# Sliding-window attention into a GELU layer: batch 0 loaded and worked on pair by pair, first weights in three column pieces

## The chip, the cores and the metric

The kernel runs on one core of a Trainium2 chip. Time is device time in microseconds (us) of that core. Three runs of the kernel before gave 296.78, 296.99 and 299.27 us, median 296.99. A separate execution was recorded with the profiler: it took 296.65 us, of which the recorded span of instructions is 294.6 us.

## The reference

The input is q, k and v of eight batches, eight heads, 576 positions and 64 values a head, and two weight matrices, w_in (512 x 2048) and w_out (2048 x 512), all in float32.

```python
scores = scale * np.matmul(q, k.transpose(0, 1, 3, 2))
mask = np.abs(pos[:, None] - pos[None, :]) <= 32
attn = softmax(where(mask, scores, -1e9))
attn_out = np.matmul(attn, v)                       # 8, 8, 576, 64
x = attn_out.transpose(0, 2, 1, 3).reshape(4608, 512)
out = gelu_tanh(x @ w_in) @ w_out                   # 4608, 512
```

## The kernel before, in words

**Tiles and stages.** The 4608 rows of x are worked on in nine tiles of 512 rows (`t`), and the attention of a later batch is woven between the products of an earlier tile. The products run in fp16. For tile `t`, the first product x @ w_in gives 16 blocks of 128 columns of the hidden layer (`fc`), each a sum of four matmuls of 512 columns, one for each quarter `dc` of d_model; a GELU on ScalarE follows. A quarter `dc` of x is what the pair of heads `dc` gives, so the matmuls with `dc` 0 can begin when pair 0 of the attention is done. The second product takes the hidden layer to the output.

**The start.** Nothing can be woven into the attention of batch 0, so it and the first product of tile 0 make a start of their own (lines 796 to 920). Each pair of heads passes these steps, which the code calls by name:

- `cast_early`: q and k of the pair become fp16 (VectorE for q, GpSimd for k).
- `turn` and `trans_out`: eight transposes on TensorE into PSUM banks x0 and x1, and two copies out of them (QT and KT).
- `score`: the scores of the pair, with a bias matmul that brings the mask, and one `Exp` of 128 x 1024 on ScalarE (line 481).
- `sum_up` and `invert`: the sums of the rows by a matmul with ones (line 495), then `Ln` and `Exp` on ScalarE (lines 530, 531), which give 1/sum.
- `values`: v of the pair becomes fp16 (GpSimd) and is copied once more, shifted by 64 rows (`pair_v` on VectorE, lines 225, 226).
- `times` and `spread`: the products with v (line 505), and the product with 1/sum, which writes the pair's quarter of x (line 540).

The order before is: all of q and k are loaded, then v pair by pair, then w_in; scores and sums of all four pairs go first, then `finish` (`times` and `spread`) pair by pair as v lands. `spin` issues matmuls on zeros whose result nobody reads.

**Weights of the first product.** w_in is loaded in fp32 in eight DMAs of 128 x 1024 (two column halves `x`, four quarters `dc`, line 246), becomes fp16 in casts of 512 columns (line 250) on GpSimd and ScalarE or VectorE, and is used as a view `w_cols` in which a block `fc` takes every fourth column of a group of 512. w_out's rows are loaded to match, four consecutive rows to a partition. `block_in(ns, *dcs)` issues the matmuls (line 577) of blocks `ns` for quarters `dcs`; after the last quarter come the GELUs. Before, blocks 0 to 5 are run quarter by quarter as w_in's first half arrives, then 6 and 7, then 8 to 13, then 14 and 15.

**What sets the order.** The order is written out by hand: every engine takes its instructions in the order of the program, and SP's queue, which issues nearly all loads, takes the DMAs in that order too. After line 920 a table of slots (`PLAN_0`) weaves the attention of batch 1 into the second product of tile 0 (line 723). The stage buffers (five, 8 KB a partition) are passed from v of batch 0 and the w_in pieces on to the pieces of w_out and v of batch 1, so a load of these waits for the last cast out of the buffer.

Of the kernel before, what the change touches and what calls it, by code (L numbers as in the profile page):

```python
# [9 lines left out]
FP32 = mybir.dt.float32  # L10
# [68 lines left out]
def kernel(  # L79
# [152 lines left out]
            copy(V[0:64, 3 + c, :, :], V[0:64, c, :, :])  # L232

    w_in_v = moe_w_in.rearrange("(c p) f -> p c f", p=128)
    w_out_v = moe_w_out.rearrange("(i p c) f -> i p c f", p=128, c=4)
    w_cols = w_in16.rearrange("k d (i p j) -> k d i j p", i=4, j=4)

    def stage_w():
        return stage.tile([128, 4, 512], FP32, name="wst", tag="stage")

    wi = {}

    def load_w_in(x, dc):
        if dc % 2 == 0:
            wi[x, dc // 2] = stage.tile([128, 2, 1024], FP32, name="wst", tag="stage")
        nc.sync.dma_start(wi[x, dc // 2][:, dc % 2, :], w_in_v[:, dc, 1024 * x:1024 * x + 1024])

    def cast_w_in(x, dc, *copies):
        for y, copy in enumerate(copies):
            copy(w_in16[:, dc, 1024 * x + 512 * y:1024 * x + 512 * y + 512],  # L250
                 wi[x, dc // 2][:, dc % 2, 512 * y:512 * y + 512])

    def load_w_out(i, w, c0=0, c1=4):
        nc.sync.dma_start(w[:, c0:c1, :], w_out_v[i, :, c0:c1, :])
        return w

    def cast_w(w, dst, on_dve=(0, 1), cs=range(4), on_act=()):
# [5 lines left out]
    qk(0, (nc.sync, nc.scalar))  # L263
    tails_0("k")
    qk(2, (nc.scalar, nc.sync))
    qk(4)
    qk(6)
    load_table(exp_set)
    def v_of_pair(g, hs=(0, 1)):
        for h in (2 * g + x for x in hs):  # L270
            nc.sync.dma_start(raws[0][3][:, :, h, :], v[0, h, 0:512, :].rearrange("(c p) d -> p c d", p=128))

    vs(4)
    for g in range(3):
        v_of_pair(g)
    for x in range(2):
        load_w_in(0, x)
        v_of_pair(3, (x,))
    for x, dc in ((0, 2), (0, 3), (1, 0), (1, 1), (1, 2), (1, 3)):
        load_w_in(x, dc)  # L280

    idle = KTs[1][:, 0, 0:512]
    nc.vector.memset(idle, 0.0)
# [1 line left out]
    def spin(n, width=512, ps=None):  # L285
        ps = psO.tile([128, 512], FP32, name="spin", tag="O") if ps is None else ps
        for _ in range(n):
            nc.tensor.matmul(ps[:, 0:width], idle[:, 0:128], idle[:, 0:width], start=True, stop=True)
# [43 lines left out]
    def cast_early(b, pr, engs):  # L332
        for src, dst, eng in zip(raws[b][0:2], halfs[b][0:2], engs):
            if eng is not None:
                eng.tensor_copy(dst[:, pr, :, :, :].rearrange("p j h d -> p h j d"),
                                src[:, 2 * pr:2 * pr + 2, :].rearrange("p h (j d) -> p h j d", j=4))
# [26 lines left out]
    def cast_tail_0(copy, i):  # L363
        if len(halfs[0]) < 3:
            halfs[0].append(hp.tile([128, H, 64], FP16, name="t16", tag="t16"))
        copy(halfs[0][2][:, 4 * i:4 * i + 4, :], raws[0][2][:, 4 * i:4 * i + 4, :])
# [21 lines left out]
    def trans_out(b, pr, pt, ptk, copy=nc.vector.tensor_copy):  # L388
        nc.vector.tensor_copy(QTs[b][:, pr, :, 0:128], pt[:, 0:4, :])
        copy(  # L390
            KTs[b % 2][:, pr, :].rearrange("d (p j) -> d p j", j=4),
            ptk[:, 0:4, :].rearrange("d j p -> d p j"))
# [165 lines left out]
    def ffn_in(t, n, d0=0, d1=4, then=True):  # L558
        fc = column(t, n)
        if t not in gTs:  # L560
            gTs[t] = gp.tile([128, NF, 512], FP16, name="gT", tag="gT")
        if d0 == 0:
            if t == 0:
                i = n % 8
                if i in (4, 6):
                    phs["S"] = psS.tile([128, 2, 512], FP32, name="ph2", tag=f"S{i // 2 - 2}")
                phs[fc] = psO.tile([128, 512], FP32, name="ph", tag="DO"[i]) if i < 2 else \
                    bank(i - 2) if i < 4 else phs["S"][:, i % 2, :]
            else:
                i = 3 if n in (1, 2) else 0 if n == 0 else (2, 1, 0)[n % 3] if t < NT - 2 else (2, 0)[n % 2 if n > 3 else 0]  # L570
                if n == 1:
                    phs["S"] = psS.tile([128, 2, 512], FP32, name="ph3", tag="S0")
                phs[fc] = bank(i) if i < 2 else phs["S"][:, n - 1, :] if i == 3 else \
                    psO.tile([128, 512], FP32, name="ph", tag="D")
        ph = phs[fc]
        for dc in range(d0, d1):
            nc.tensor.matmul(ph, w_cols[:, dc, fc // 4, fc % 4, :],  # L577
                             xT[:, dc, t * 512 % RING:t * 512 % RING + 512],
                             start=(dc == 0), stop=(dc == 3))
        if d1 == 4 and then:  # L580
            gelu(t, n)
# [9 lines left out]
    def in_w(eng, unit, *which):  # L591

        i, j = UNITS[unit] // 2, 2 * (UNITS[unit] % 2)
        A11, A12, A21, A22 = (w_cols[:, d:d + 2, c + i, j:j + 2, :] for c in (0, 2) for d in (0, 2))
        if (unit, "s") not in mixed:
            halves = [(rawp if unit == "A" else yp).tile([128, 2, 2, 2, 128], FP16, name="wc" + unit + str(x),
                                                         tag=("qr", "kr")[x] if unit == "A" else "yo") for x in range(2)]
            mixed[unit, "s"] = [half[:, x] for half in halves for x in range(2)]
        S1, S2, S3, S4 = mixed[unit, "s"]
        mixed[unit, "w"] = dict(A11=A11, A12=A12, A22=A22, S1=S1, S2=S2, S3=S3, S4=S4)  # L600
        for x in which:
            dst, a, b, op = ((S1, A21, A22, ALU.add), (S2, S1, A11, ALU.subtract),
                             (S3, A11, A21, ALU.subtract), (S4, A12, S2, ALU.subtract))[x - 1]
            eng.tensor_tensor(dst, a, b, op=op)
# [195 lines left out]
    def turn(g):  # L800
        pts[g] = (bank16(0), bank16(1))
        trans_pair(0, g, *pts[g], now=False)

    def pieces(tag, name):
        return psO.tile([128, 512], FP32, name=name, tag=tag) if tag in "OD" else \
            psS.tile([128, 2, 512], FP32, name=name, tag=tag)[:, 0, :]

    lts, os = {}, {}

    def sums_of(g):  # L810
        d = pieces("DO"[g % 2], "ps_d")
        sum_up(0, g, d, groups[(0, g)])
        lts[g] = invert(0, g, d)


    cast_early(0, 0, split)
    turn(0)
    trans_out(0, 0, *pts[0], nc.scalar.copy)
    cast_early(0, 1, split)
    cast_tail_0(nc.vector.tensor_copy, 1)  # L820
    spin(3)
    trans_tail_0(psO.tile([128, 8, 128], FP16, name="pt", tag="D"), 1, nc.scalar.copy)
    score(0, 0, 0)
    turn(1)
    cast_early(0, 2, split)
    trans_out(0, 1, *pts[1])
    spin(1)
    sums_of(0)
    cast_early(0, 3, split)
    turn(2)  # L830
    score(0, 1, 1)
    trans_out(0, 2, *pts[2])
    cast_vt(0)
    spin(1)
    score(0, 2, 0)
    turn(3)
    trans_out(0, 3, *pts[3])
    sums_of(1)
    score(0, 3, 1)
    sums_of(2)  # L840

    def values(g, copy):
        hs = slice(2 * g, 2 * g + 2)
        copy(Vs[0][:, 0:4, hs, :], raws[0][3][:, :, hs, :])
        pair_v(0, nc.vector.tensor_copy, hs)

    def finish(g, o):
        times(0, g, o, groups.pop((0, g)))
        spread(0, g, o, lts[g])

    values(0, nc.gpsimd.tensor_copy)
    values(1, nc.gpsimd.tensor_copy)

    qk, tails, vs = load_early(1)
    qk(0)
    wo = [load_w_out(0, stage_w())]
    qk(2)

    finish(0, bank(0))
    finish(1, bank(1))  # L860
    s0 = psS.tile([128, 2, 512], FP32, name="ps_o", tag="S0")
    spin(2, 512, s0[:, 1, :])
    sums_of(3)
    spin(2, 512, s0[:, 1, :])
    values(2, nc.gpsimd.tensor_copy)
    s1 = psS.tile([128, 2, 512], FP32, name="ps_o", tag="S1")
    finish(2, s1[:, 0, :])
    six = range(6)

    def block_in(ns, *dcs):  # L870
        for dc in dcs:
# [2 lines left out]
        if 3 in dcs:  # L874
            for n in ns:
                gelu(0, n)

    cast_w_in(0, 0, nc.gpsimd.tensor_copy, nc.scalar.copy)
    values(3, nc.vector.tensor_copy)
    block_in(six, 0)  # L880
    cast_w_in(0, 1, nc.gpsimd.tensor_copy, nc.scalar.copy)
    block_in(six, 1)
    finish(3, s1[:, 1, :])
    load_table(gelu_set)
    cast_w_in(0, 2, nc.gpsimd.tensor_copy, nc.scalar.copy)
    cast_w_in(0, 3, nc.gpsimd.tensor_copy, nc.vector.tensor_copy)
    block_in(six, 2, 3)
    band_out()
    for dc in range(4):
        cast_w_in(1, dc, nc.vector.tensor_copy, nc.gpsimd.tensor_copy)  # L890
    wo.append(load_w_out(1, stage_w()))
    qk(4)
    tails_0("q")
    wo.append(load_w_out(2, stage_w(), 0, 2))
# [10 lines left out]
    cast_open(1)  # L905
    split = (nc.gpsimd, nc.vector)

    block_in((6, 7), 0, 1, 2, 3)
    block_in(range(8, 14), 0, 1, 2, 3)
    cast_early(1, 0, split)  # L910
    cast_w(wo[0], w_out16[:, 0:4, :], (0,), (0, 2, 3, 1))
    for dc in range(4):
# [197 lines left out]
```

## Time and profile before

| what | value |
|---|---|
| runs | 296.78, 296.99, 299.27 us; median 296.99 |
| profiled execution, its own time | 296.65 us |
| its span | 294.6 us |
| TensorE matmul busy in the span | 285.9 us, 97% |
| VectorE, ScalarE, GpSimd busy | 72%, 67%, 30% |
| first useful matmul of the first product | 17.37 us |
| first matmul of the second product | 32.69 us |

The page cuts the span into 40 slices of 7.4 us. TensorE has idle time in the first three slices and in the last; from 21 us on the start is one unbroken row of matmuls. The two times in the last rows are from the timeline of TensorE and are used below as marks: everything that this change touches lies ahead of the second one, but for the order of columns in the weights.

### The profile page before, as it was taken

How to read it: one execution, taken by the hardware profiler on the slowest of the kernel's cores; microseconds unless marked ns; L12 is line 12 of the kernel's file. 1: busy time of each engine (PE TensorE's matmuls, PEld its weight loads, DVE VectorE, ACT ScalarE, POOL GpSimd, SP SyncE). 2: the span in 40 equal slices, each digit the busy share in tenths (PEclk: the TensorE clock that was granted, in tenths of full speed). 3: DMA queues.
4: the chain of work that ended last, by engine and by line, in shares of the span. 5: the costliest groups of instructions: out<-in, count | busy, mean ns of one | idle time of the engine just before them, and what ended most of it. 6: DMA issues, size and time to landing. Idle time of an engine off the chain costs nothing.

```text
span 294.6 us, 7286 instructions
## 1 busy us (share of the span) xinstructions
PE 285.9 (97%) x2945; PEld 192.7 (65%) x2945; DVE 212.4 (72%) x467; ACT 196.5 (67%) x315; POOL 88.8 (30%) x143
## 2 busy tenths in 40 slices
PE   8889999999999999999999999999999999999993
PEld 3535545547765687568755885588558867887783
DVE  4755477998897667858796878686957877865762
ACT  5965877777677874787667776796669558706800
POOL 4445335004228713205250615050800050025000
PEclk9999999999999999999999999999999999999998
DMA  7999998999999998999999999899691040004013
GB/s 229 275 380 396 359 305 196 254 186 203 248 229 202 251 202 188 113 139 245 162 212 94 246 157 191 116 245 154 117 190 7 0 118 28 2 26 120 0 47 99
DMA packets 114392, 51.02 MB, mean 173 GB/s; under 512 B 98471, under 2 KB 110247, under 8 KB 114102
## 3 DMA queue, kind: packets, MB, share of 16 engines
q1 hardware_dynamic: 89460, 38.67, 62.4%
q0 software_dynamic: 23776, 10.83, 23.4%
q10 hardware_dynamic: 1122, 1.06, 1.1%
q8 instruction: 23, 0.38, 0.6%
q14 instruction: 11, 0.09, 0.1%
HBM read 36.70 MB, written 9.44 MB: 157 GB/s over the span
## 4 chain that ended last, share of the span: by engine, by line
PE 85%; DVE 5%; DMA 5%; issue 1%; SPq 1%; ACT 1%; POOL 0%; DVEq 0%
PE mm L751 32%; PE ph L577 17%; PE mm L577 16%; PE ps_s L468 4%; PE pu L629 3%; DMA kr<-in_k_dram 3%; PE mm L723 2%; DMA wst<-in_moe_w_in_dram 2%; PE py L723 2%; PE ps_d L495 2%; PE ps_o L505 2%; DVE t L684 2%; DVE s L694 1%; PE mm L629 1%; PE ps_od L495 1%; PE ps_od L505 1%
## 5 line engine op out<-in xcount | busy, mean ns | idle before, releaser
L577 PEld LDWEIGHTS <-w_in 128*128 128x128 f16 x512 | 57.4, 113 | 49.8 <-POOL w_in L250 1.5
L577 PE MATMUL ph<-xT,w_in 128*128 128x512 f16 x256 | 64.5, 379 | 0.6 <-POOL w_in L250 0.6
L577 PE MATMUL mm<-xT,w_in 128*128 128x512 f16 x256 | 64.1, 379 | 0.0
L585 ACT ACTIVATE gT<-mm 128x512 f16<-128x512 f32 x60 | 35.6, 598 | 33.3 <-PE mm L577 32.7
L713 POOL DMA_DIRECT2D out_dram<-y x55 | 32.8, 605 | 82.4 <-DVE y L780 75.3
L751 PEld LDWEIGHTS <-s 128*128 128x128 f16 x512 | 49.3, 98 | 7.1 <-DVE s L694 0.6
L751 PE MATMUL mm<-t,s 128*128 128x256 f16 x376 | 45.2, 273 | 0.2 <-DVE y L764 0.2
L694 DVE TENSOR_TENSOR s<-gT 128x512 f16<-128x512 f16 x64 | 27.5, 430 | 19.1 <-ACT gT L585 18.9
L751 PEld LDWEIGHTS <-gT 128*128 128x128 f16 x384 | 36.2, 98 | 6.4
L585 ACT ACTIVATE gT<-ph 128x512 f16<-128x512 f32 x58 | 32.4, 604 | 10.9 <-PE ph L577 10.9
L481 ACT ACTIVATE pe<-ps_s 128x960 f16<-128x960 f32 (+1 forms) x31 | 29.5, 975 | 13.2 <-PE ps_s L468 13.1
L751 PE MATMUL mm<-w_out,gT 128*128 128x256 f16 x256 | 32.6, 273 | 0.0
L104 ACT ACT_TABLE_LOAD x18 | 23.1, 1283 | 2.2 <-issue 1.9
L530 ACT ACTIVATE lt<-ps_d 128x480 f32<-128x480 f32 (+2 forms) x28 | 15.6, 556 | 10.4 <-PE ps_d L495 6.9
L531 ACT ACTIVATE lt<-lt 128x480 f32<-128x480 f32 (+3 forms) x36 | 21.1, 585 | 1.1
L490 DVE TENSOR_TENSOR pe<-pe,band 128x960 f16<-128x960 f16 x28 | 18.5, 680 | 2.0 <-ACT pe L481 1.9
L505 PEld LDWEIGHTS <-V 128*64 128x64 f16 x520 | 13.7, 111 | 5.5 <-DVE V L226 1.5
L751 PE MATMUL mm<-t,gT 128*128 128x256 f16 x128 | 16.1, 273 | 0.0
L694 DVE TENSOR_TENSOR s<-s,gT 128x512 f16<-128x512 f16 x32 | 14.0, 436 | 1.1
L216 POOL DMA_DIRECT2D V<-in_v_dram x16 | 14.3, 908 | 1.1 <-PE ps_s L468 0.4
L751 PE MATMUL mm<-w_out,s 128*128 128x256 f16 x120 | 14.6, 273 | 0.0
L540 DVE TENSOR_TENSOR xT<-ps_o,lt 128x480 f16<-128x480 f32 (+5 forms) x26 | 13.4, 535 | 1.6 <-PE ps_o L505 1.6
(149 smaller groups left out, 390.3 us busy)
## 6 DMA issues: line engine op xcount, KB each, us to landing
kr<-in_k_dram SPq DMA_DIRECT2D x31, 256.0 KB, 10.2
qr<-in_q_dram SPq DMA_DIRECT2D x6, 1024.0 KB, 5.9
wst<-in_moe_w_in_dram SPq DMA_DIRECT2D x8, 512.0 KB, 6.6
wst<-in_moe_w_out_dram SPq DMA_DIRECT2D x2, 1024.0 KB, 10.5
wst<-in_moe_w_out_dram SPq DMA_DIRECT2D x4, 512.0 KB, 7.4
qr<-in_v_dram SPq DMA_DIRECT2D x8, 256.0 KB, 6.5
V<-in_v_dram POOLq DMA_DIRECT2D x16, 128.0 KB, 8.5
qr<-in_q_dram SPq DMA_DIRECT2D x7, 256.0 KB, 7.3
```

Of the source, the lines that this page charges most:

```text
L104: nc.scalar.add_instruction(mybir.InstLoadActFuncSet(name=nc.get_next_instruction_name(), act_func_set_id=which, ins=[], outs=[]))
L216: nc.gpsimd.dma_start(V[:, c, :, :], v[b, :, 128 * c:128 * c + 128, :].rearrange("h p d -> p h d"))
L481: nc.scalar.activation(pe, ps[:, :, 0:w], AF.Exp, scale=SCALE)
L490: nc.vector.tensor_tensor(pe, pe, m.rearrange("k (o j) p -> k o j p", o=1).broadcast_to(list(pe.shape)), op=ALU.mult)
L505: nc.tensor.matmul(o[64 * h:64 * h + 64, cols].rearrange("d (j p) -> d j p", j=4)[:, :, p0 - q0:p1 - q0], Vs[b % 2][:, slot, 2 * pr + h, : ...
L530: nc.scalar.activation(lt[:, 0:n], d[:, 0:n], AF.Ln)
L531: nc.scalar.activation(lt[:, 0:n], lt[:, 0:n], AF.Exp, scale=-1.0)
L577: nc.tensor.matmul(ph, w_cols[:, dc, fc // 4, fc % 4, :], xT[:, dc, t * 512 % RING:t * 512 % RING + 512], start=(dc == 0), stop=(dc == 3))
L585: nc.scalar.activation(gTs[t][:, fc, :], phs[fc], AF.Gelu_apprx_tanh)
L694: nc.vector.tensor_tensor(dst, x, y, op=op)
L713: eng.dma_start(out_v[b, j, q0 + p:q0 + p + e, cols], yo[m:m + e, cols])
L751: nc.tensor.matmul(pys["apart"][:, 0:256] if apart else py[:, blk, :], lhsT, wino[w][:, f, :], start=(new and i % (8 if one else 16) == 0) ...
```

## The change

**Loads.** v of pair 0 (and the last 64 rows of v) is now issued ahead of q and k of pair 2, v of pair 1 ahead of q and k of pair 3. The form of the loads of v, one row to a partition, stands in line 271 of both kernels. w_in comes in twelve DMAs: pieces of 768, 768 and 512 columns for each quarter. The pieces of 512 share a buffer with those of 768. Loads for batch 1 and of w_out keep their place in SP's queue behind w_in; the second piece of w_out is now two DMAs.

**Columns.** A block takes every sixth column of a piece of 768, or every fourth of the piece of 512; w_out's rows follow. So blocks 0 to 5 need the first piece alone.

**Order of the work.** Each pair of heads goes through its scores, sums, values, `times` and `spread` before the next is begun, as far as its loads allow. Two `spin`s of two matmuls and two of one are gone, one of one remains, and one of three as before. The key copy of pair 3 goes from VectorE to ScalarE, behind the `invert` of pair 2. The first products of quarter 0 come ahead of `times` of pair 2 for five blocks; the sums of pair 3 come behind that. The cast of quarter 3 goes to GpSimd and ScalarE, ahead of the table load for GELU. Blocks 6 to 9 are interleaved by halves, then 10 and 11, then 12 and 13.

```diff
+    part = [(0, 6), (6, 6), (12, 4)]
+    def w_cols(d0, d1, fc, n):
+        f0, step = part[min(fc // 6, 2)]
+        return w_in16[:, d0:d1, 128 * f0:128 * (f0 + step)].rearrange(
+            "k d (p j) -> k d j p", j=step)[:, :, fc - f0:fc - f0 + n, :]
...
+    def w_in_of(x, dc):
+        return (wi[x, dc // 2][:, 768 * (dc % 2):768 * (dc % 2) + 768] if x < 2 else
+                wi[dc // 2, dc % 2][:, 1536:2048])
...
     def cast_w_in(x, dc, *copies):
+        w, n = w_in_of(x, dc), (768 if x < 2 else 512) // len(copies)
         for y, copy in enumerate(copies):
...
     qk(2, (nc.scalar, nc.sync))
-    qk(4)
-    qk(6)
...
     vs(4)
-    for g in range(3):
-        v_of_pair(g)
-    for x in range(2):
-        load_w_in(0, x)
-        v_of_pair(3, (x,))
-    for x, dc in ((0, 2), (0, 3), (1, 0), (1, 1), (1, 2), (1, 3)):
-        load_w_in(x, dc)
+    v_of_pair(0)
+    qk(4)
+    v_of_pair(1)
+    qk(6)
+    v_of_pair(2)
+    load_w_in(0, 0)
+    load_w_in(0, 1)
+    v_of_pair(3)
+    for dc in range(2, 4):
+        load_w_in(0, dc)
+    for x in (1, 2):
+        for dc in range(4):
+            load_w_in(x, dc)
...
+    cast_early(0, 1, split)
+    score(0, 0, 0)
+    spin(1)
+    turn(1)
+    trans_out(0, 1, *pts[1])
+    sums_of(0, pieces("D", "ps_d"))
+    score(0, 1, 1)
+    values(0)
+    cast_vt(0)
+    weigh_0(0, pieces("D", "ps_o"))
+    cast_early(0, 2, split)
+    spread(0, 0, os[0], lts[0])
+    turn(2)
+    trans_out(0, 2, *pts[2])
+    sums_of(1, pieces("O", "ps_d"))
+    score(0, 2, 0)
+    values(1)
+    cast_early(0, 3, split)
+    weigh_0(1, pieces("O", "ps_o"))
+    spread(0, 1, os[1], lts[1])
+    turn(3)
+    sums_of(2, pieces("D", "ps_d"))
+    trans_out(0, 3, *pts[3], nc.scalar.copy)
+    score(0, 3, 1)
+    values(2)
     cast_w_in(0, 0, nc.gpsimd.tensor_copy, nc.scalar.copy)
-    values(3, nc.vector.tensor_copy)
-    block_in(six, 0)
+    block_in((0, 2, 3, 4, 5), 0)
     cast_w_in(0, 1, nc.gpsimd.tensor_copy, nc.scalar.copy)
-    block_in(six, 1)
-    finish(3, s1[:, 1, :])
+    values(3)
+    s1 = psS.tile([128, 2, 512], FP32, name="ps_o", tag="S1")
+    weigh_0(2, s1[:, 0, :])
+    sums_of(3, s1[:, 1, :])
+    spread(0, 2, os[2], lts[2])
+    block_in((1,), 0)
+    cast_w_in(0, 2, nc.gpsimd.tensor_copy, nc.scalar.copy)
+    block_in((0, 2, 3, 4, 5, 1), 1)
+    weigh_0(3, s1[:, 1, :])
+    spread(0, 3, os[3], lts[3])
+    cast_w_in(0, 3, nc.gpsimd.tensor_copy, nc.scalar.copy)
     load_table(gelu_set)
-    cast_w_in(0, 2, nc.gpsimd.tensor_copy, nc.scalar.copy)
-    cast_w_in(0, 3, nc.gpsimd.tensor_copy, nc.vector.tensor_copy)
-    block_in(six, 2, 3)
+    block_in((0, 1, 2, 3, 4, 5), 2, 3)
     band_out()
...
-    wo.append(load_w_out(1, stage_w()))
+    for dc in range(4):
+        cast_w_in(2, dc, (nc.vector.tensor_copy, nc.gpsimd.tensor_copy)[dc % 2])
+    wo.append(load_w_out(1, stage_w(), 0, 2))
+    load_w_out(1, wo[1], 2, 4)
...
-    block_in((6, 7), 0, 1, 2, 3)
-    block_in(range(8, 14), 0, 1, 2, 3)
+    block_in((6, 7), 0, 1)
+    block_in((8, 9), 0, 1)
+    block_in((6, 7), 2, 3)
+    block_in((8, 9), 2, 3)
+    block_in((10, 11), 0, 1, 2, 3)
+    block_in((12, 13), 0, 1, 2, 3)
```

More of the change, by code (lines that the diff above doesn't have):

```diff
@@ L234 @@
     w_in_v = moe_w_in.rearrange("(c p) f -> p c f", p=128)
-    w_out_v = moe_w_out.rearrange("(i p c) f -> i p c f", p=128, c=4)
-    w_cols = w_in16.rearrange("k d (i p j) -> k d i j p", i=4, j=4)
+    part = [(0, 6), (6, 6), (12, 4)]
[3 more added lines that the diff above has]
+            "k d (p j) -> k d j p", j=step)[:, :, fc - f0:fc - f0 + n, :]
     def stage_w():
@@ L241 @@
     wi = {}
+    def w_in_of(x, dc):
+        return (wi[x, dc // 2][:, 768 * (dc % 2):768 * (dc % 2) + 768] if x < 2 else
+                wi[dc // 2, dc % 2][:, 1536:2048])
     def load_w_in(x, dc):
-        if dc % 2 == 0:
-            wi[x, dc // 2] = stage.tile([128, 2, 1024], FP32, name="wst", tag="stage")
-        nc.sync.dma_start(wi[x, dc // 2][:, dc % 2, :], w_in_v[:, dc, 1024 * x:1024 * x + 1024])
+        if x < 2 and dc % 2 == 0:
+            wi[x, dc // 2] = stage.tile([128, 2048], FP32, name="wst", tag="stage")
+        nc.sync.dma_start(w_in_of(x, dc), w_in_v[:, dc, 768 * x:768 * x + (768 if x < 2 else 512)])
     def cast_w_in(x, dc, *copies):
+        w, n = w_in_of(x, dc), (768 if x < 2 else 512) // len(copies)
         for y, copy in enumerate(copies):
-            copy(w_in16[:, dc, 1024 * x + 512 * y:1024 * x + 512 * y + 512],
-                 wi[x, dc // 2][:, dc % 2, 512 * y:512 * y + 512])
+            copy(w_in16[:, dc, 768 * x + n * y:768 * x + n * y + n], w[:, n * y:n * y + n])
     def load_w_out(i, w, c0=0, c1=4):
-        nc.sync.dma_start(w[:, c0:c1, :], w_out_v[i, :, c0:c1, :])
+        f = 4 * i + c0
+        f0, step = part[min(f // 6, 2)]
+        rows = moe_w_out[128 * f0:128 * (f0 + step), :].rearrange("(p c) f -> p c f", c=step)
+        nc.sync.dma_start(w[:, c0:c1, :], rows[:, f - f0:f - f0 + c1 - c0, :])
         return w
@@ L576, in ffn_in @@
         for dc in range(d0, d1):
-            nc.tensor.matmul(ph, w_cols[:, dc, fc // 4, fc % 4, :],
+            nc.tensor.matmul(ph, w_cols(dc, dc + 1, fc, 1)[:, 0, 0, :],
                              xT[:, dc, t * 512 % RING:t * 512 % RING + 512],
@@ L593, in in_w @@
         i, j = UNITS[unit] // 2, 2 * (UNITS[unit] % 2)
-        A11, A12, A21, A22 = (w_cols[:, d:d + 2, c + i, j:j + 2, :] for c in (0, 2) for d in (0, 2))
+        A11, A12, A21, A22 = (w_cols(d, d + 2, 4 * (c + i) + j, 2) for c in (0, 2) for d in (0, 2))
         if (unit, "s") not in mixed:
@@ L808, with sums_of, values, weigh_0 @@
     lts, os = {}, {}
-    def sums_of(g):
-        d = pieces("DO"[g % 2], "ps_d")
+    def sums_of(g, d):
         sum_up(0, g, d, groups[(0, g)])
         lts[g] = invert(0, g, d)
[L816 to L842, printed above, removed]
+    def values(g):
         hs = slice(2 * g, 2 * g + 2)
-        copy(Vs[0][:, 0:4, hs, :], raws[0][3][:, :, hs, :])
+        nc.gpsimd.tensor_copy(Vs[0][:, 0:4, hs, :], raws[0][3][:, :, hs, :])
         pair_v(0, nc.vector.tensor_copy, hs)
-    def finish(g, o):
+    def weigh_0(g, o):
+        os[g] = o
         times(0, g, o, groups.pop((0, g)))
[L849 to L868, printed above, removed]
     def block_in(ns, *dcs):
@@ L876, in block_in @@
                 gelu(0, n)
+    cast_early(0, 0, split)
+    turn(0)
+    trans_out(0, 0, *pts[0], nc.scalar.copy)
+    cast_tail_0(nc.vector.tensor_copy, 1)
+    spin(3)
+    trans_tail_0(psO.tile([128, 8, 128], FP16, name="pt", tag="D"), 1, nc.scalar.copy)
+    cast_early(0, 1, split)
[23 more added lines that the diff above has]
+    values(2)
     cast_w_in(0, 0, nc.gpsimd.tensor_copy, nc.scalar.copy)
-    values(3, nc.vector.tensor_copy)
-    block_in(six, 0)
+    block_in((0, 2, 3, 4, 5), 0)
     cast_w_in(0, 1, nc.gpsimd.tensor_copy, nc.scalar.copy)
-    block_in(six, 1)
-    finish(3, s1[:, 1, :])
+    values(3)
[9 more added lines that the diff above has]
+    cast_w_in(0, 3, nc.gpsimd.tensor_copy, nc.scalar.copy)
     load_table(gelu_set)
-    cast_w_in(0, 2, nc.gpsimd.tensor_copy, nc.scalar.copy)
-    cast_w_in(0, 3, nc.gpsimd.tensor_copy, nc.vector.tensor_copy)
-    block_in(six, 2, 3)
+    block_in((0, 1, 2, 3, 4, 5), 2, 3)
     band_out()
+    qk, tails, vs = load_early(1)
+    qk(0)
+    wo = [load_w_out(0, stage_w())]
+    qk(2)
     for dc in range(4):
         cast_w_in(1, dc, nc.vector.tensor_copy, nc.gpsimd.tensor_copy)
-    wo.append(load_w_out(1, stage_w()))
+    for dc in range(4):
+        cast_w_in(2, dc, (nc.vector.tensor_copy, nc.gpsimd.tensor_copy)[dc % 2])
+    wo.append(load_w_out(1, stage_w(), 0, 2))
+    load_w_out(1, wo[1], 2, 4)
     qk(4)
```

## The prediction

> **What bounds the kernel now.** I read the busy time by stretches first, then the timeline of TensorE from 12 to 33 us, then what GpSimd and ScalarE waited for there, and last the chain that ended last. By stretches (columns: length, TensorE busy and matmuls, granted clock, DMA share, GB/s):
>
> ```profile
> 14.00:17.40 3.40, 2.40 (x37) 1.00 1.10 342
> 17.40:21.00 3.60, 3.26 (x29) 1.00 1.00 395
> 21.00:33.00 12.00, 12.00 (x68) 1.00 1.04 398
> ```
>
> From 21 us on TensorE has no gap; the list of TensorE's waits names 0.4 us from there to 76 us and 0.2 us after. So a change of the start is worth just what it moves the first matmul of the second product (32.69 us, "the mark"), and that passes to the end one for one. The timeline of TensorE ahead of it:
>
> ```profile
> 17.37 0.62 PE L577 MATMUL ph<-xT,w_in 128*128 128x512 f16 x2 [0.29 <-POOL w_in L250]
> ...
> 19.20 0.62 PE L577 MATMUL ph<-xT,w_in 128*128 128x512 f16 x2 [0.34 <-POOL w_in L250]
> ...
> 20.62 0.44 PE L505 MATMUL ps_o<-pe,V 128*64 128x96 f16 x16
> ```
>
> Matmuls of 512 columns follow each other at 0.216 us (twelve in 2.59 us of the chain). The mark is then 17.37 + six (1.30) + a wait of 0.53 + six (1.30) + values of pair 3 (0.49) + twelve (2.59) + forty for the other blocks (8.64) + eight transposes (0.45) = 32.67. What it waits for is w_in and, ahead of that, the attention. GpSimd shows the landings:
>
> ```profile
> 6.65 0.61 POOL L335 CAST k<-kr 128x512 f16<-128x512 f32 x1 [1.53 <-DMA kr<-in_k_dram]
> 8.14 0.61 POOL L335 CAST k<-kr 128x512 f16<-128x512 f32 x1 [0.88 <-DMA kr<-in_k_dram]
> 10.13 0.61 POOL L335 CAST k<-kr 128x512 f16<-128x512 f32 x1 [1.38 <-DMA kr<-in_k_dram]
> ...
> 11.93 0.61 POOL L844 CAST V<-vr 128x512 f16<-128x512 f32 x1 [0.40 <-DMA vr<-in_v_dram]
> 13.06 0.61 POOL L844 CAST V<-vr 128x512 f16<-128x512 f32 x1 [0.53 <-DMA vr<-in_v_dram]
> 15.40 0.62 POOL L844 CAST V<-vr 128x512 f16<-128x512 f32 x1 [1.72 <-DMA vr<-in_v_dram]
> 16.70 0.62 POOL L250 CAST w_in<-wst 128x512 f16<-128x512 f32 x1 [0.69 <-DMA wst<-in_moe_w_in_dram]
> ```
>
> and ScalarE that it is done with the last `Exp` of scores (pair 3) at 14.2 and reaches the first weights just as they land:
>
> ```profile
> 13.17 1.01 ACT L481 ACTIVATE pe<-ps_s 128x1024 f16<-128x1024 f32 x1
> ...
> 16.30 0.63 ACT L531 ACTIVATE lt<-lt 128x512 f32<-128x512 f32 x1
> 16.84 0.60 ACT L250 CAST w_in<-wst 128x512 f16<-128x512 f32 x1
> ```
>
> In the chain SP's queue itself is a link: the issue of v at 10.10 waited for a key load issued eight DMAs before it.
>
> ```profile
> 4.94 5.14 DMA kr<-in_k_dram
> ```
>
> **Part 1, landings.** The loads are one stream. From the rows: q and k of a pair take 1.5 us (6.65 to 8.14); a load of v of one head 0.57 (13.06 - 11.93, for two) to 0.75 us (10.13 to 15.40 for seven such loads); a quarter of w_in of 1024 columns 1.29 us (20.30 to 21.59), so 0.97 for 768 and 0.64 for 512. In the new order, from k of pair 1 at 6.6: v of pair 0 with the tail of v (three such loads) 8.7 to 9.0; k of pair 2 at 10.2 to 10.6 (before 8.1); v of pair 1 at 11.6 to 12.0; k of pair 3 at 13.1 to 13.6 (before 10.1); v of pair 2 at 14.6 to 15.3; w_in's first piece at 15.5 to 16.3, 16.5 to 17.3, 18.8 to 19.3 and 19.8 to 20.3 (before 16.6, 18.5, 20.2, 21.5). So the last quarter is 1.2 to 1.7 us earlier and the last keys 3.0 to 3.5 us later. No issue waits longer than this: with eight loads in flight each one's eighth predecessor has landed.
>
> **Part 2, the engines.** Instruction by instruction with the earlier landings, every duration from a row of before and 0.03 us for a handover (the same sums with the landings of before give 32.7 for the mark, so they are not biased there):
>
> - k of pair 2: cast 0.61, transposes from 10.87, key copy on VectorE (0.68, behind the query copy) until 12.18, scores until 12.61, `Exp` 12.71 to 13.71 (ScalarE is busy with 1/sum of pair 1 until then).
> - k of pair 3: landed 13.1, cast until 13.74, transposes until 14.0. Sums of pair 2 stand behind these: 14.01 to 14.39.
> - ScalarE, in its order: `Ln` and `Exp` of pair 2 until 15.67, the key copy of pair 3 (0.59) until 16.20; only then scores of pair 3 until 16.63, `Exp` 16.66 to 17.66, and its half of the cast of w_in (384 columns, 0.48 from 0.60 for 512) until 18.1.
> - So the first product begins at **18.12** instead of 17.37, though GpSimd's half of the cast is ready at 16.0.
>
> From there TensorE is dense: five matmuls 1.08, values of pair 2 0.40, sums of pair 3 0.23, one matmul 0.22, six 1.30, values of pair 3 0.40, twelve 2.59, forty 8.64, transposes 0.45: 33.4. The wait of 0.53 us is gone, but 0.63 us of values and sums stand now behind the first product instead of ahead of it. With the later landings the sum is 33.9. Against 32.69 that is +0.7 to +1.2; I take **+1.0 us**.
>
> **Part 3, what is hidden.** The cast of quarter 3 is ready at 22.1 (ScalarE, behind 1/sum of pair 3) and `spread` of pair 3 at 22.6, for a use at 23.0; bare, each costs its lateness. The table load ends at 23.4 and two GELUs at 24.6, for banks needed at 25.2. VectorE's casts of the second piece come behind `band_out` (1.3 us) at 24.1, 24.4, 24.7, 25.0, for uses from 24.3: the tightest cover, 0.2 us. Third piece: ready by 27, used at 29.5. The spins taken out filled waits only, so they return nothing. The loads for batch 1 have as many bytes ahead of them as before; the second piece of w_out now waits for a cast at about 25.5 (issued at 24.17 before), with some 2 MB, 5 us at 398 GB/s, queued in front; before, its cast began at 35.1 and its use at 37.1, and that use moves by +1.0. Uncovered it costs at most 1.3.
>
> **Part 4, columns.** A weight load now steps over six fp16 values (12 bytes) in three of four blocks; no row shows that step. The nearest rows are steps of one and four:
>
> ```profile
> L629 PEld LDWEIGHTS <-w_in x48: 112/113/116, 240.5 to 274.8; 128*128 128x128 f16 x48
> L629 PEld LDWEIGHTS <-wcA x32: 95/98/98, 243.3 to 275.4; 128*128 128x128 f16 x32
> ```
>
> 15 ns for three more values of step, so 10 more for two more: 123 ns (estimate), behind matmuls of 216 ns: nothing. At the 40 matmuls of 256 columns with such weights (0.109 us apart), 10 ns each would be 0.4 us. From below, step one (98 ns) saves nothing either, as these matmuls keep 0.109 with both rows. I take 0, range 0 to +0.4. The eight mixed-weight sums on VectorE (0.68 us each, line 604) are off the chain; if each took twice that, VectorE (72% busy) has room.
>
> The Trainium skill speaks against this step: "SBUF — State Buffer", Door 1, says that reads want two or more hits in a 16-byte line, and six fp16 values give four reads in three lines (it also calls eight values free). By the stricter reading a load might double to some 226 ns (estimate from the 113 above), 10 ns over the 216 in 384 loads and 117 over in 40: +8.5 us. No row here shows a doubling, and the step of four already halves the hits for 15 ns.
>
> **Rivals.**
>
> *TensorE's clock falls.* The first eight matmuls of the program are slow:
>
> ```profile
> 1.26 3.59 PE L288 MATMUL spin<-KT 128*128 128x512 f16 x8 [1.26 <-DVE KT L283]
> ```
>
> 0.45 us each, against 0.216 later; eight lose 1.86 us. The emptiest 3.4 us before (14.0 to 17.4) still hold 2.4 us of work, with spins, and stay fast. In the new order TensorE has 0.3 us of work from 14.5 to 18.1, with no spin. If that is empty enough, the first product starts slow: +1.0 + 1.9 = **+2.9 us**. For it: the stretch; against it: it is hardly longer than the 3.6 us that the start needed to turn fast. "TensorE: Matmul & The Clock Gate", Part 1, puts the limit at one idle window of some 3.4 us, free-running, so that only a window falling wholly into the stretch would do it; the trace has no case.
>
> *The weights decide (faster).* If the last quarter's landing sets the mark as it does now, quarter 3's six matmuls start at 21.0 (landing 20.3, cast, handover) instead of 22.3: **-1.3 us**. It decides when `Exp` of pair 3 ends by 16.9 us, 0.75 ahead of my sum; the gain then grows with the lead. For it: DMA is what the chain of before runs through ahead of 18.5 us. Against it: even with all landings 1.5 us earlier than my early ones the engines alone give 33.0, +0.3.
>
> *A wait that I don't see*, as in the tightest covers or the weight loads of Part 4: +1.5 to +3.
>
> **The numbers.** The forecast has 0.5 (+0.3 to +1.8), the clock 0.25 (+2.2 to +3.7), the faster case 0.17 (-0.3 to -1.8), an unseen wait 0.08. On the profiled execution +1.0 gives a span of 295.6 and 297.65 us; that execution lies 0.34 below the median, so on the median **298.0**. The range from 295.6 to 300.0 takes in most of the faster case and half of the clock's; left out is about 0.17. A measurement of this kernel can tell about 1% (3 us) from no change: slower by that needs the upper part of the clock or of an unseen wait, 0.15; faster 0.03; within 0.82.
>
> **What would show it.** Right: first line-577 matmul at 17.7 to 18.6, released by ScalarE's cast; last `Exp` of scores ending at 17.2 to 18.2; first matmul of the second product at 33.0 to 34.4; no wait of TensorE after it. Wrong: matmuls of 0.43 us spacing after 17 us (clock); the first product ahead of 17 us with waits for w_in DMAs (weights); weight loads over 130 ns (columns).

## The result, and the profile after

The changed kernel took 300.75 us (median of ten runs, 299.98 to 301.92); the kernel before, run beside it, 297.74 us (296.57 to 299.60). The ratio is 1.010, with a 95% interval from 1.007 to 1.0131: slower by 3.0 us. The forecast was 298.0, in a range up to 300.0: the sign was right, the size (+1.0 us) was a third of what came, and the time lies 0.75 us outside the range. The forecast stood on the median of three earlier runs, 296.99; beside the changed kernel the kernel before took 0.75 us more than that, and a rise of 3.0 us from 296.99 would have ended at the edge of the range. Ratios here and below leave out runs more than 1.5% above the fastest of their kernel: three of `e5_pieces`, one of `f2_pieces_spins`, one of the kernel before (301.29 us).

The profiled execution took 301.92 us with a span of 300.2 us, 5.6 us more than the span before. The mark, the first matmul of the second product, went from 32.69 to 37.60 us (+4.9), and TensorE waits nowhere behind it for longer than before; the other 0.7 us lie behind the last VectorE instruction, where the last stores land (4.8 us to the end of the span instead of 4.2). The busy time by stretches (length, TensorE busy and matmuls, granted clock, DMA share, GB/s) shows at once what is new:

```profile
14.70:18.20 3.50, 1.11 (x25) 1.00 1.09 338
18.20:25.00 6.80, 6.08 (x30) 0.50 1.04 395
25.00:37.60 12.60, 12.47 (x77) 1.00 1.07 365
```

From 18.2 to 25.0 us the granted clock is 0.50; before, it was 1.00 in every stretch from 14.0 to 33.0. That is the rival (TensorE's clock falls) which the prediction gave a chance of 0.25. The timeline of TensorE around it (the sums of pair 2, the scores of pair 3, the first products, and matmuls after the return of the clock):

```profile
14.64 0.41 PE L510 MATMUL ps_d<-pe,ones 128*64 128x512 f16 x2
...
16.88 0.42 PE L483 MATMUL ps_s<-QT,KT 64*64 64x96 f16 x16 [1.49 <-ACT KT L405]
...
18.92 0.60 PE L592 MATMUL ph<-xT,w_in 128*128 128x512 f16 x1 [1.63 <-ACT w_in L259]
19.32 1.06 PE L592 MATMUL mm<-xT,w_in 128*128 128x512 f16 x2
...
26.06 0.59 PE L592 MATMUL mm<-xT,w_in 128*128 128x512 f16 x2
```

Two matmuls take 1.06 us at first and 0.59 later: 0.43 us apart, the sign that the prediction named for the clock. Both waits ahead of them are for ScalarE. On ScalarE, the key copy of pair 3 behind `invert`, the last `Exp` of scores, and the casts behind that, where they stood in the forecast's sum:

```profile
15.72 0.63 ACT L546 ACTIVATE lt<-lt 128x512 f32<-128x512 f32 x1
16.25 0.57 ACT L405 COPY KT<-pt 128x512 f16<-128x512 f16 x1
17.35 1.02 ACT L496 ACTIVATE pe<-ps_s 128x1024 f16<-128x1024 f32 x1 [0.53 <-PE ps_s L483]
18.27 0.92 ACT L259 CAST w_in<-wst 128x384 f16<-128x384 f32 x2
```

The landings, seen as before by GpSimd's casts (k of pairs 2 and 3, v of pair 2, then the first and the last quarter of w_in):

```profile
10.67 0.79 POOL L350 CAST k<-kr 128x512 f16<-128x512 f32 x1 [0.16 <-DMA kr<-in_k_dram]
...
13.29 0.96 POOL L350 CAST k<-kr 128x512 f16<-128x512 f32 x1 [0.89 <-DMA kr<-in_k_dram]
14.49 0.61 POOL L831 CAST V<-vr 128x512 f16<-128x512 f32 x1 [0.23 <-DMA vr<-in_v_dram]
15.39 0.51 POOL L259 CAST w_in<-wst 128x384 f16<-128x384 f32 x1 [0.28 <-DMA wst<-in_moe_w_in_dram]
...
20.87 0.51 POOL L259 CAST w_in<-wst 128x384 f16<-128x384 f32 x1 [0.47 <-DMA wst<-in_moe_w_in_dram]
```

The last quarter of the first piece is cast from 20.87 instead of 21.59, the last keys from 13.29 instead of 10.13, and the first quarter of w_in lies on the chip 3.5 us before TensorE can use it. Weight loads with a step of six (most of them) beside the step of one:

```profile
L644 PEld LDWEIGHTS <-w_in x48: 112/125/126, 245.4 to 279.8; 128*128 128x128 f16 x48
L644 PEld LDWEIGHTS <-wcA x32: 95/98/98, 248.3 to 280.4; 128*128 128x128 f16 x32
```

The eight small mixed-weight sums on VectorE went from 0.68 to 0.85 us where the step is six; no wait of TensorE names them.

Each timed run also has a mean granted clock of its own. Of the ten runs of the changed kernel two have 0.994 (spans 298.4 and 298.2 us), three 0.989 to 0.990 (299.0, 298.5, 298.3), five 0.984 or 0.985 (300.2, 299.9, 300.0, 299.1, 299.7). The ten executions of this document that have a kept trace, one for each kernel, say how to read such a mean: the four whose clock holds through the start have 0.995 to 1.000, the five in which it is down for 3.4 us there (called a period below) have 0.990 to 0.994, and the one with 6.8 us, the one shown, has 0.985. By this reading the clock fell in all ten runs, in some for one period and in some for two. The execution shown is among the latter and 1.2 us above its median, and the profiled one of before (296.65 us) is 1.1 below the median beside it: so the times of these two differ by 5.3 us (their spans by 5.6) where the medians differ by 3.0.

### The profile page after: what moved, and what is told of

It is laid out like the page before. It is cut to its first block, busy times and chain, and to the rows that moved or that the text cites. A ratio compares the mean times of both kernels' runs of the same rounds, so it can differ in the third digit from the quotient of the medians.

```text
span 300.2 us, 7294 instructions
## 1 busy us (share of the span) xinstructions
PE 287.6 (96%) x2940; PEld 196.9 (66%) x2940; DVE 212.5 (71%) x466; ACT 197.4 (66%) x317; POOL 91.5 (30%) x146
## 3 DMA queue, kind: packets, MB, share of 16 engines
q10 hardware_dynamic: 1122, 1.06, 1.1%
## 4 chain that ended last, share of the span: by engine, by line
PE 73%; DMA 12%; SPq 7%; DVE 5%; issue 1%; ACT 1%; POOL 0%; ACTq 0%; DVEq 0%
PE mm L766 32%; PE mm L592 15%; PE ph L592 13%; DMA wst<-in_moe_w_in_dram 4%; DMA wst<-in_moe_w_out_dram 4%; PE pu L644 3%; PE ps_s L483 3%; PE ps_d L510 2%; SPq L196 2%; PE ps_o L520 2%; DMA qr<-in_q_dram 1%; SPq L265 1%; DMA kr<-in_k_dram 1%; DVE s L709 1%; PE mm L644 1%; DVE t L699 1%
## 5 line engine op out<-in xcount | busy, mean ns | idle before, releaser
L592 PEld LDWEIGHTS <-w_in 128*128 128x128 f16 x512 | 62.0, 123 | 48.2 <-issue 2.6
L592 PE MATMUL ph<-xT,w_in 128*128 128x512 f16 x256 | 65.9, 387 | 1.8 <-ACT w_in L259 1.6
L709 DVE TENSOR_TENSOR s<-gT 128x512 f16<-128x512 f16 x64 | 27.5, 430 | 19.8 <-ACT gT L600 19.6
L555 DVE TENSOR_TENSOR xT<-ps_o,lt 128x480 f16<-128x480 f32 (+5 forms) x28 | 14.8, 547 | 5.0 <-PE ps_o L520 2.6
L483 PE MATMUL ps_s<-QT,KT 64*64 64x128 f16 (+3 forms) x576 | 13.5, 216 | 1.8 <-ACT KT L405 1.5
L483 PEld LDWEIGHTS <-KT 64*64 64x64 f16 x576 | 9.8, 106 | 8.0 <-issue 4.0
```

Of the source, the lines that this page charges most:

```text
L483: nc.tensor.matmul(sides[h][64 * half:64 * half + 64, 4 * n * r:4 * n * r + 4 * n].rearrange("k (j p) -> k j p", j=4)[:, :, p0 - q0:p1 - q ...
L592: nc.tensor.matmul(ph, w_cols(dc, dc + 1, fc, 1)[:, 0, 0, :], xT[:, dc, t * 512 % RING:t * 512 % RING + 512], start=(dc == 0), stop=(dc == 3))
L709: nc.vector.tensor_tensor(dst, x, y, op=op)
```

## The experiments

All were timed against the kernel before on the same chip. Theory A: the fallen clock costs most of the difference, and the longer chain of ScalarE ahead of the first product the rest.

**Matmuls on zeros in both waits** (`e1_spins`).

```diff
     sums_of(2, pieces("D", "ps_d"))
+    spin(6)
     trans_out(0, 3, *pts[3], nc.scalar.copy)
     score(0, 3, 1)
+    spin(6)
     values(2)
```

> The changed kernel with twelve matmuls on zeros: six ahead of the scores of pair 3, six behind them; each six take 1.3 us and fit into waits of 1.5 and 1.6 us. Theory A (the fallen clock costs 3.4 of the 4.9 us at the mark, the longer chain of ScalarE the rest): matmuls of the first product 0.216 us apart from the first one on, first product still at 18.6 to 19.0, first matmul of the second product at 33.9 to 34.3 instead of 37.6, time 1.0 to 1.5 us above the kernel before. Rival B (the order of the work and the landings cost all of it, the slow matmuls only fill time in which the weights would be awaited anyway): the mark stays at 37 or later and the time 3 us above before.

Ratio to before 1.0048 (1.0025 to 1.0071): 1.4 us above it instead of 3.0. Twelve more matmuls make the kernel faster by half of its loss. By stretches, and the first products:

```profile
14.70:18.80 4.10, 3.81 (x36) 1.00 1.07 344
18.80:25.00 6.20, 6.18 (x57) 1.00 1.04 397
25.00:34.30 9.30, 9.30 (x50) 1.00 1.05 386
```

```profile
18.82 0.39 PE L592 MATMUL ph<-xT,w_in 128*128 128x512 f16 x1 [0.22 <-ACT w_in L259]
19.04 0.59 PE L592 MATMUL mm<-xT,w_in 128*128 128x512 f16 x2
...
34.34 0.59 PE L738 MATMUL mm<-w_out,gT 128*128 128x512 f16 x2
```

The first product begins where it did (18.82 against 18.92), yet the mark comes at 34.34 instead of 37.60. In this pair of executions the clock is worth 3.2 to 3.3 us, about half of the 6.8 us that it was down. B falls: the quarters of w_in are cast within 0.1 us of where they were (15.31, 17.77, 19.83 and 20.81 us, against 15.39, 17.82, 19.90 and 20.87), and the faster matmuls bring the mark forward by all that they save. The mark is still 1.65 us later than before.

**Key copy of pair 3 on VectorE** (`e2_kcopy`).

```diff
-    trans_out(0, 3, *pts[3], nc.scalar.copy)
+    trans_out(0, 3, *pts[3])
```

> The changed kernel with the key copy of pair 3 back on VectorE, so that it does not stand behind the 1/sum of pair 2 on ScalarE; no matmul added. Worked out from the rows: scores of pair 3 at 15.7 instead of 16.9, its Exp ending at 17.2 to 17.4 instead of 18.4, first product at 17.6 to 18.0. Theory A: the empty stretch of TensorE is 0.9 us shorter and broken in its middle; if the clock stays up the mark is at 33.0 to 33.2 and the time 0.3 to 0.6 us above before, if it falls all the same 3.4 us more. Rival C (landings of the weights, not ScalarE, hold the first product): first product stays at 18.9.

Ratio 1.0004 (0.9975 to 1.0033): this one argument gives the loss back. The first product begins at 17.61, 1.3 us earlier, and the mark is at 34.76; C falls. The clock still falls, but for one period, not for the two that the expectation priced at 3.4 us:

```profile
14.70:17.60 2.90, 0.91 (x24) 1.00 1.10 331
17.60:18.80 1.20, 1.19 (x5) 0.96 1.04 396
18.80:22.20 3.40, 3.40 (x25) 0.51 1.02 398
22.20:24.00 1.80, 1.80 (x23) 1.00 1.06 394
```

The reader is to see the order in time: the bare stretch ends at 17.6, five matmuls run fast, and only then does the clock go down, for 3.4 us. So this edit changes two things: of the 2.8 us by which the mark comes earlier, 1.3 are the shorter chain of ScalarE, and the rest is about one period of slow clock less. Among the twelve runs three have a mean clock of 1.000 and a median of 297.14 us, nine have 0.994 or less and a median of 298.11.

**The kernel before without six of its matmuls on zeros** (`e4_before_nospin`).

```diff
-    spin(1)
...
-    spin(1)
...
-    spin(2, 512, s0[:, 1, :])
     sums_of(3)
-    spin(2, 512, s0[:, 1, :])
```

> The kernel before without six of its matmuls on zeros (one, one, two and two; the eight and the three at the very start stay). Theory A: TensorE's barest stretch, 14.8 to 17.4 us, then holds 0.6 us of work in 2.6 us; it is shorter than in the changed kernel, so the clock may stay up: then the mark is at 32.7 and the time within 0.3 us of before; if such a stretch is enough, the first product starts at 0.43 us a matmul and the time is 1.7 to 3.4 us above before. The prediction's own step (these matmuls only fill waits and return nothing when taken out) expects no gain in either case.

Ratio 1.0026 (0.9997 to 1.0055): a rise of 0.8 us, less than the 1.7 to 3.4 expected for a fall, and alone it would leave the question open. The trace does not:

```profile
14.70:17.40 2.70, 0.69 (x19) 1.00 1.11 345
17.40:18.20 0.80, 0.80 (x4) 0.94 0.92 349
18.20:21.40 3.20, 3.20 (x9) 0.50 1.01 402
```

The first product begins at 17.39, as in the kernel before, then the clock falls and the mark is at 33.85, 1.2 us late: one period at half speed costs 1.7, and 0.5 of it falls into the wait for w_in that the kernel before has there. The twelve runs say the same: all have a mean clock of 0.994 or less, against six of the 59 runs of the kernel before that were timed beside the experiments. So the matmuls on zeros were holding the clock up; the same stretch before, with them, has 2.0 us of work in 2.6 us.

**One half of the matmuls on zeros** (`e6_spin_first`, `e7_spin_second`): one of the two additions of `e1_spins` each.

> The changed kernel with six matmuls on zeros ahead of the scores of pair 3 only; the wait of 1.6 us behind those scores stays empty. Asks how bare a stretch has to be. If a stretch of some 1.7 us with nothing in it is harmless, the mark is at 34.3 as with all twelve, and the time 1.4 us above before; if the clock falls all the same, by one period of 3.4 us at half speed (1.7 us lost), the mark is at 36 and the time as in the changed kernel or up to 1 us below it.

> The changed kernel with six matmuls on zeros behind the scores of pair 3 only; the wait of 1.5 us ahead of them stays empty. TensorE is then busy without a break from 16.9 us on, with 1.7 us of near emptiness ahead. Expected as for the other half: mark at 34.3 if this is harmless, 36 with one period at half speed; with the two halves alike, the fall needs both waits, with one worse, it is that one.

Ratios 1.009 (1.0064 to 1.0115) and 1.0083 (1.0055 to 1.0111), from four runs each: nearly the changed kernel's loss; marks at 35.75 and 35.50, near the 36 expected for one period. In the first the clock falls behind the second wait, in the second behind the first wait, each for one period. The two fences are of `e6_spin_first` and of `e7_spin_second`:

```profile
17.00:18.60 1.60, 0.07 (x8) 1.00 1.05 388
18.60:19.20 0.60, 0.50 (x3) 1.00 1.00 389
19.20:22.60 3.40, 3.40 (x25) 0.51 1.04 403
```

```profile
14.70:16.80 2.10, 0.61 (x12) 0.99 1.12 312
16.80:20.10 3.30, 3.30 (x25) 0.50 1.03 391
```

In these two executions a wait of 1.5 or 1.6 us with next to nothing in it was enough, in the midst of denser work, and each wait did it by itself. It does not do so every time: by the mean clocks two of the four runs of `e6_spin_first` (0.995 and 0.996) and one of `e7_spin_second` (0.999) kept the clock up. Half of the cover brings the mark forward by 1.9 to 2.1 us against the changed kernel; the times, of four runs each, don't show it.

**The weights' part alone** (`e5_pieces`): the kernel before with the pieces, the columns and the order of blocks 6 to 13.

```diff
+    part = [(0, 6), (6, 6), (12, 4)]
...
-            wi[x, dc // 2] = stage.tile([128, 2, 1024], FP32, name="wst", tag="stage")
+            wi[x, dc // 2] = stage.tile([128, 2048], FP32, name="wst", tag="stage")
...
-    block_in((6, 7), 0, 1, 2, 3)
-    block_in(range(8, 14), 0, 1, 2, 3)
+    block_in((6, 7), 0, 1)
...
```

> The kernel before with the weights' part of the change alone: w_in in pieces of 768, 768 and 512 columns, a step of six columns in a block, blocks 6 to 13 in the changed kernel's order; attention, loads of q, k, v and the matmuls on zeros as before. Worked out: last quarter of the first piece lands 1.2 us earlier, the first product begins at 17.4 as before because ScalarE reaches its first cast then, and its wait of 0.5 us goes: mark at 32.0 to 32.2, time 0.5 us below before (0 to -1.0). Rival (the step of six columns costs): weight loads well over 125 ns or matmuls more than 0.216 us apart, time above before.

Ratio 0.9992 (0.9960 to 1.0024), but from two groups: six runs from 295.92 to 297.69, six from 298.91 to 301.31. The profiled execution (298.99) is of the upper group: v of pair 1 is cast at 15.32 instead of 13.06, the clock is down from 17.2 to 20.6, the mark is at 35.92. The clock does not make the upper group by itself: two of its six runs have a mean clock of 0.998 (298.91 us) and 1.000 (299.16 us). The step does no harm: in `e1_spins` and `f1_dve_casts`, which have it too, eighteen matmuls with it follow each other in 3.89 and 3.88 us, 0.216 each (here in 4.10). So the rival of the step falls, while a gain of the pieces is neither shown nor excluded.

**The weights' part with five more matmuls on zeros** (`f2_pieces_spins`).

```diff
     finish(0, bank(0))
+    spin(2)
...
     sums_of(3)
-    spin(2, 512, s0[:, 1, :])
+    spin(5, 512, s0[:, 1, :])
```

> The kernel before with the weights' part of the change, and five more matmuls on zeros in the waits for v (two behind the values of pair 0, three behind the sums of pair 3). Without these the runs fell into two groups, 295.9 to 297.7 and 298.9 to 301.3 us. Theory A (the upper group is those executions in which the clock falls): the upper group goes and the median comes to 296.5 to 297.2, 0.5 to 1.0 us below before. Rival (late landings of v make the upper group by themselves): the two groups stay.

Ratio 1.0019 (1.0001 to 1.0037): eleven runs from 297.04 to 299.24, one at 301.83, median 297.71. The upper group thins out, but the gain that A expects does not come. The profiled execution keeps the clock at 1.00 through the start, and yet its first product begins at 18.66 and its mark is at 33.82, 1.1 us late. Its trace shows late v: v of pair 1 is cast from 13.94 instead of 13.06, the last products with it begin at 15.54 instead of 14.36, the sums of pair 3 behind it at 16.41 instead of 15.22, and `Ln`, `Exp` and the cast of w_in on ScalarE follow. The two matmuls added ahead of this end at 14.4, before v is cast; the three added behind the sums end before ScalarE has cast the weights. So the rival is right at least in part: late v costs time without the clock, and the run at 299.24 us has a mean clock of 1.000.

**A mended version of the change** (`f1_dve_casts`).

```diff
     sums_of(2, pieces("D", "ps_d"))
-    trans_out(0, 3, *pts[3], nc.scalar.copy)
+    spin(3)
+    trans_out(0, 3, *pts[3])
...
-    cast_w_in(0, 0, nc.gpsimd.tensor_copy, nc.scalar.copy)
+    cast_w_in(0, 0, nc.gpsimd.tensor_copy, nc.vector.tensor_copy)
...
-    cast_w_in(0, 1, nc.gpsimd.tensor_copy, nc.scalar.copy)
+    cast_w_in(0, 1, nc.gpsimd.tensor_copy, nc.vector.tensor_copy)
```

> The changed kernel mended where the runs so far point: key copy of pair 3 on VectorE, VectorE instead of ScalarE for its half of the casts of quarters 0 and 1 (so that they do not wait for the last Exp of scores), three matmuls on zeros ahead of the scores of pair 3. Theory A with the chain of ScalarE as second cause: first product at 16.5 to 17.0 instead of 18.9, no slow matmuls, mark at 32.3 to 32.9, time 0 to 0.5 us below before. If instead the landings of w_in hold the start, the first product stays at 17.8 or later and the mark at 33.5 or later.

Ratio 0.9980 (0.9963 to 0.9997), median 296.54 against 297.12: 0.6 us below the kernel before and some 3.5 us below the change as it was made. The clock stays up (all twelve runs have a mean of 0.997 or more), though the first stretch is none too full:

```profile
14.70:17.20 2.50, 1.47 (x27) 1.00 1.09 335
17.20:25.00 7.80, 7.66 (x64) 1.00 1.04 391
25.00:32.90 7.90, 7.90 (x44) 1.00 1.05 390
```

The first product begins at 17.27, later than the 16.5 to 17.0 expected. Two things end there together: GpSimd's cast of w_in's first quarter (16.45 to 17.21) and the last `Exp` (16.22 to 17.24), which the trace names as the releaser. The mark is at 32.95, 0.05 past its range and 0.26 behind the kernel before, in an execution whose span (294.4 us) is 0.2 below that one's. So the gain of 0.6 us is that of the timed runs; the two profiles don't show its place.

## Why the prediction was wrong, step by step

**What bounds, and the mark: right.** TensorE waits for nothing new behind the mark, and the change is worth what it moves it: +4.9 of 5.6 us in the profiled execution, with 0.7 at the very end.

**Landings: right within 1 us.** Foretold 10.2 to 10.6 for k of pair 2, 13.1 to 13.6 for k of pair 3, 15.5 to 16.3 and 19.8 to 20.3 for the first and last quarter of w_in; seen 10.67, 13.29, 15.39 and 20.87. The last quarter is 0.7 us earlier than before, where 1.2 to 1.7 were foretold.

**The engines: right in mechanism, short in size.** The first product was foretold for 18.12 and for +0.7 to +1.2 us at the mark with the clock up; `e1_spins` shows 18.82, a mark 1.65 later and a time 1.4 us above before. The order was as worked out (key copy behind 1/sum, `Exp`, cast), and `e2_kcopy` shows that it is the cause: without that link the product begins 1.3 us earlier. Most of the missing 0.7 us stands ahead of ScalarE: the sums of pair 2 begin at 14.64 (14.55 in `e1_spins`) where the sum had 14.01. They stand behind the transposes of k of pair 3, whose cast, put at 13.1 and 0.61 us long, began at 13.29 and took 0.96.

**"The spins taken out filled waits only, so they return nothing": the step that failed.** It priced these matmuls at zero (six taken out, one put in elsewhere: five fewer) because TensorE did not need their result or their time. `e4_before_nospin` shows that they held the clock: without them it falls for 3.4 us and the mark is 1.2 us late. `e1_spins` shows that twelve such matmuls in the new waits give 3.3 of the 4.9 us at the mark back.

**The clock rival: right in mechanism, but argued down by a condition that does not hold, and priced too small.** Its argument against itself was that the stretch is hardly longer than 3.6 us and that a window of 3.4 us must fall wholly into it. The runs show that a wait of 1.6 us with 0.07 us of work can be enough (`e6_spin_first`), and that the fall can come up to 1.1 us after work has begun again (`e2_kcopy`). And the price of 1.86 us was that of one slow period; the execution shown has two, 6.8 us at 0.50, and loses 3.3. The Trainium skill, "TensorE: Matmul & The Clock Gate", Part 1, has the length right (about 3.4 us; 3.4 here, once or twice) and the condition, one idle window, too strict: ahead of every fall at the start, in the executions profiled, TensorE had 0.97 us or more of work in 3.4 us.

**What is hidden: right but for one cover.** The casts of the second piece, named as the tightest, came late in the execution shown: a weight load waited 0.56 us for one, and eighteen matmuls took 4.19 us that take 3.88 in `f1_dve_casts`.

**Columns: right.** 125 ns against an estimate of 123, and hidden behind matmuls 0.216 us apart. The doubling to 226 ns, the prediction's estimate from the stricter reading of "SBUF — State Buffer", Door 1, in the Trainium skill, is refuted by the rows for weight loads; on VectorE the step of six does cost 0.17 us an instruction. (A step of four leaves two of eight values in that page's 16-byte line, a quarter and not the half that the prediction names.)

**The faster case** did not come. With ScalarE's key copy and casts out of the way and three matmuls on zeros to hold the clock (`f1_dve_casts`), the same loads make a kernel that is 0.2% faster than before; the -1.3 us at the mark is seen in no run.

**Open.** Why v of pair 1 landed 2 us late in `e5_pieces` and 0.9 in `f2_pieces_spins`. Also what else spreads the runs of the kernel before: by their mean clocks it loses its clock in six of 59 (298.14 to 301.29 us, means of 0.985 to 0.994), but runs of 300.06 and 300.15 us have 1.000.

## What to carry to other kernels

Ask of every instruction that is taken out what state it kept, not only whose time it took: a matmul that nobody reads can be the cheapest thing in the kernel when it keeps the clock up. When a change moves waits of TensorE, add up its work in every stretch of 3.4 us and compare with the barest one that the trace shows at full clock; below that, price the fall at one and at two periods. And when loads come earlier, look next at which in-order engine stands between them and their use: here a copy ahead of an `Exp` on ScalarE and a cast behind it put the first product 1.5 us later, though its weights had landed in time.

## What the hardware showed that was not expected

The clock did not need an empty window: 0.69 us of work in 2.7 us were too little (`e4_before_nospin`) and 0.91 in 2.9 too (`e2_kcopy`), while 1.47 in 2.5 (`f1_dve_casts`) and 2.0 in 2.6 (before) were enough, in the executions profiled. The ten traces come into one order when the work is added up over the length that the clock stays down, 3.41 us:

| execution | clock at the start | TensorE busy in 3.41 us |
|---|---|---|
| changed kernel | fell | 0.97 us, just ahead of the fall |
| `e5_pieces` | fell | 0.97 us |
| `e4_before_nospin` | fell | 1.40 us |
| `e2_kcopy` | fell | 1.52 us |
| `e6_spin_first` | fell | 1.70 us |
| `e7_spin_second` | fell | 1.85 us |
| `f2_pieces_spins` | held | 2.22 us, the barest from 6 us on |
| `f1_dve_casts` | held | 2.23 us |
| kernel before | held | 2.38 us |
| `e1_spins` | held | 2.73 us |

So in these executions the clock fell with 1.85 us of work or less, and held with 2.22 or more; where between them the limit lies was not measured. Once down, it stayed down for 3.4 us in the five executions in which TensorE was busy throughout, and for 6.8 in the one in which the first 0.67 us were still empty (18.25 to 18.92, changed kernel); one case does not show that this is the reason. By its mean clocks (0.984 to 0.994) the changed kernel did both.
